# Linear attention before two expert layers: the attention of the last twelve tiles in pairs

## The chip, the cores and the metric

The kernel runs on one core of one Trainium2 chip. The metric is the device time of one execution in microseconds, the median of several runs. One more execution is recorded by the hardware profiler; all rows come from that one.

The engines of a core work side by side, each in its own order, and wait for one another through semaphores: PE (TensorE) multiplies matrices, DVE (VectorE), ACT (ScalarE) and POOL (GpSimd) work element by element, SP (SyncE) issues most DMAs. PEld is the loading of weights into PE's array, which runs beside the products.

## The reference

Three stages, over 4 batches, 8 heads, 768 time steps and head width 48:

```python
# attention, for each batch and head: state is a 48x48 matrix
for t in range(768):
    y[t]  = r[t] @ (state + outer(u * k[t], v[t]))
    state = w[:, None] * state + outer(k[t], v[t])
# x: 3072 rows of 384
h = maximum(maximum(x @ w1, x @ w2), x @ w3);  x = h @ w_out          # width 768
xn = x / rms(x) * rms_g
out = (silu(xn @ w_gate) * (xn @ w_val)) @ w_out2                      # width 1536
```

## The kernel before

**Attention in tiles.** The recurrence is computed in chunks of 128 time steps; a tile `i` is one chunk of one batch, `i = 4*chunk + batch`, 24 tiles in all. For a tile there are, on PE: the scores `pe_a` (L352: eight small products of 48 rows, for four pairs of heads, the two heads of a pair on two halves of the rows, into two PSUM banks), the outputs `pe_y` (L410: products with 32 output columns, four side by side, into one bank) and, but for the last chunk, the state products `pe_st` (L378: 64 output columns, two side by side, one bank). Each product shows as two instructions in the profile. Around them: `prep` scales r and k by the decay (L316, DVE) and forms `ru = r*u*k` (L324 and L325, on DVE for tiles under 8, on POOL later); `prep_b` sums `ru` by head (L332, DVE) and spreads the sums on diagonals (`Dg`, L335, POOL); `mix` copies the masked scores into `Dg` (L359, DVE, two instructions); `fin` takes the outputs out of PSUM (L425 on ACT, L426 on DVE); `mask_kv` takes the state products out (L365, ACT, into the buffer `kv`); POOL decays the state and adds `kv` (L384, L386). From tile 8 on a part of `fin`'s output goes into a buffer `yt` and four DMAs turn it into place (`turn`, L438 and L439).

**Order of the work.** Everything is written out in one order. The first expert layer is cut into `slots` (24 for each chunk `u`; 18 of them are nine products `pl` of 128x512 in one of four PSUM banks `psm`, L99 to L101). Attention is a list of `steps`, three for each tile, which are strewn between the slots: of the stages `u` = 1 to 4 each has 12 steps, and after slot `n` the steps up to number ceil(12 (n+1) / 20) have been issued. After each step one more waiting load is issued. The step `block(i)` holds, in PE's order, scores of tile `i+1`, outputs of tile `i`, states of tile `i`. Other work goes in between: `tick` converts the experts' weights (L137 to L147), `sums_step` forms sums of weights (L168), `later` holds low parts (L498) back by a slot.

**Buffers.** The tags `ru` and `kv` have one buffer each, `yt` one, `Dg` two, `tm` and `raw` (the loaded tile) three. Scores, outputs and state products turn in the four PSUM banks of `psx`. `csb` holds the identity (used once, by the transposes of `tables3`), the mask and two columns. The tag `wf` turns in six buffers of the weight conversion.

After attention the second expert layer runs from products of sums (`px`, `pa`, L1031 and others) to the end.

Of the kernel before, what the change touches and what calls it, by code (L numbers as in the profile page):

```python
# [71 lines left out]
def rwkv_moe_kernel(ctx, tc, rkT, rkv, wd, ub, cst, rg, w1p, wo1p, w2p, out):  # L72
# [154 lines left out]
                    fn(i + off)  # L227


    csb = tp.tile([128, 259], F32, name="csb")  # L230
    ident = csb[:, 0:128]
    cmask = csb[:, 128:256].bitcast(U32)
    m01 = csb[:, 256:257], csb[:, 258:259]
    small = tp.tile([128, 4, NP], F32, name="small")
    wsb, wcl, w128, ok = (small[:, n] for n in range(4))
    usb = tp.tile([128, DM], F32, name="usb")
# [14 lines left out]
    def load_tile(i):  # L251
        if i >= NT:
            return
        a = raws[i % 3][:, :, 0:512].rearrange("p s (q t) -> p s q t", t=128)
        t = tp.tile([128, VO + NP * 144], F32, tag="tm", bufs=3, name=f"tm{i}")
        raw_t[i], tm_t[i] = a, t
        for j in range(2):
            loads.append(lambda j=j: sync.dma_start(a[64 * j:64 * j + 48], rkT[i, 48 * j:48 * j + 48]))
        rk = t[:, 0:2 * KO].rearrange("p (s n) -> p s n", s=2)[:, :, 0:DM]
        loads.append(lambda: sync.dma_start(rk, rkv[i, :, 0:2 * DM].rearrange("p (s n) -> p s n", s=2)))  # L260
        loads.append(lambda: sync.dma_start(t[:, VO:], rkv[i, :, 2 * DM:]))
# [56 lines left out]
    def prep(i):  # L318
        prep_raw(i)
        s = st[i]  # L320
        tm = s["tm"]
        ru = tp.tile([128, DM], F32, tag="ru", name=f"ru{i}")
        eng = dve if i < NRU else pool
        eng.tensor_tensor(out=ru, in0=tm[:, 0:DM], in1=usb, op=ALU.mult)  # L324
        eng.tensor_tensor(out=ru, in0=ru, in1=tm[:, KO:KO + DM], op=ALU.mult)  # L325
        s["ru"] = ru
# [18 lines left out]
    def pe_a(i):  # L345
        s = st[i]
        raw = s["raw"]
        pa = [psx.tile([128, NP, 128], F32, tag="x", name=f"pa{i}_{j}") for j in range(2)]
        for pr in range(NP):
            for j in range(2):  # L350
                sl = slice(64 * j, 64 * j + 48)
                pe.matmul(pa[j][:, pr], raw[sl, 1, pr], raw[sl, 0, pr], start=True, stop=True)  # L352
        s["pa"] = pa

    def mix(i):
        s = st[i]
        dg = s["Dg"].rearrange("p (r j) t -> p r j t", j=2)
        for j in range(2):
            dve.copy_predicated(out=dg[:, :, j], mask=cmask.unsqueeze(1).to_broadcast([128, NP, 128]),  # L359
                                data=s["pa"][j])  # L360
# [3 lines left out]
            sl = slice(48 * j, 48 * j + 48)  # L364
            act.activation(o[:, :, sl], pk, AF.Copy, scale=m01[j])  # L365

    def pe_st(i):
        s = st[i]
        c, b = divmod(i, B)
        if c == NB - 1:  # L370
            return
        tm = s["tm"]
        v3 = tm[:, VO:].rearrange("p (r q e) -> p r q e", q=3, e=D)
        pk = psx.tile([128, NP, D], F32, tag="x", name=f"pkv{i}")
        for pr in range(NP):
            for j in range(2):
                o = KO + 96 * pr + 48 * j
                pe.matmul(pk[64 * j:64 * j + 64, pr], tm[:, o:o + 64], v3[:, pr, 2 * j], start=True, stop=True)  # L378
        if c == 0:
            mask_kv(Tst[b], pk)  # L380
        else:
            kv = tp.tile([128, NP, 96], F32, tag="kv", name=f"kv{i}")
            mask_kv(kv, pk)
            pool.tensor_tensor(out=Tst[b], in0=Tst[b],  # L384
                               in1=w128.unsqueeze(2).to_broadcast([128, NP, 96]), op=ALU.mult)
            pool.tensor_tensor(out=Tst[b], in0=Tst[b], in1=kv, op=ALU.add)  # L386

    def pe_y(i):
        s = st[i]
        c, b = divmod(i, B)  # L390
        tm = s["tm"]
        py = s["py"] = psx.tile([128, 3, 128], F32, tag="x", name=f"py{i}")
        lanes = []
        for n in range(4):
            lane = []
            for k in range(3):
                m = (n + TURN[k] * (i >= TURNED)) % 4
                pr, o = (k, 32 * m) if m < 3 else (3, 32 * k)
                ops = [(tm[:, VO + 144 * pr + 48 * j + o:VO + 144 * pr + 48 * j + o + 32],
                        s["Dg"][:, 2 * pr + j]) for j in range(2) if o != (64, 0)[j]]  # L400
                if c > 0:
                    ops.append((Tst[b][:, pr, o:o + 32], s["raw"][:, 0, pr]))
                for m, (l, r) in enumerate(ops):
                    lane.append((py[32 * n:32 * n + 32, k], l, r, m == 0, m == len(ops) - 1))
            lanes.append(lane)
        for m in range(max(map(len, lanes))):
            for lane in lanes:
                if m < len(lane):
                    o, l, r, start, stop = lane[m]
                    pe.matmul(o, l, r, start=start, stop=stop)  # L410
# [3 lines left out]
    def fin(i):  # L414
        s = st[i]
        u, m = divmod(i, B)
        if m == 0:
            xt[u] = ap_.tile([128, 2, 3, 512], F32R, tag="x", bufs=2, name=f"x{u}")
        xh, xl = xt[u][:, 0], xt[u][:, 1]
        o = 128 * m  # L420
        cs = slice(o, o + 128)
        y = s["py"]

        def split(hi, lo, y):
            act.copy(hi, y)  # L425
            dve.tensor_tensor(out=lo, in0=y, in1=r32(hi), op=ALU.subtract)  # L426

        if i < TURNED:
            split(xh[:, :, cs], xl[:, :, cs], y)
            return  # L430
        t = tp.tile([128, 2, 2, 128], F32R, tag="yt", name=f"yt{i}")
        split(t[:, 0], t[:, 1], y[:, 0::2])
        split(xh[:, 1, cs], xl[:, 1, cs], y[:, 1])

        def turn():
            for n, k in enumerate((0, 2)):
                o = 32 * TURN[k]
                sync.dma_start(r32(xt[u][o:128, :, k, cs]), r32(t[0:128 - o, :, n]))  # L438
                sync.dma_start(r32(xt[u][0:o, :, k, cs]), r32(t[128 - o:128, :, n]))  # L439

        turns.append(turn)
# [1 line left out]
    turns = []  # L443

    def att_steps():
        def block(i):
            if i + 1 < NT:
                pe_a(i + 1)
                mix(i + 1)
            pe_y(i)  # L450
            fin(i)
            pe_st(i)
            load_tile(i + 3)

        def ahead(i):
            while turns:
                turns.pop(0)()
            if i < NT:
                load_next(2)
                prep(i)  # L460

        def ahead_b(i):
            load_next(1)
            prep_b(i)
            prep2(i)

        for i in range(NT):
            yield lambda i=i: block(i)
            yield lambda i=i: ahead(i + 2)
            yield lambda i=i: ahead_b(i + 2) if i + 2 < NT else None  # L470

    hs, sB = {}, {}

# [103 lines left out]
    with tc.manual_schedule():  # L577
# [3 lines left out]
            sync.dma_start(wsb[64 * j:64 * j + 48], wd[48 * j:48 * j + 48])  # L581
        load_tile(0)
        load_next(4)
        sync.dma_start(csb[:, 0:258], cst)
        sync.dma_start(m01[1][16:128], cst[0:112, 257:258])
        sync.dma_start(m01[1][0:16], cst[112:128, 257:258])
        act.dma_start(usb, ub.partition_broadcast(128))
# [725 lines left out]
```

## Time and profile before

| | us |
|---|---|
| median of 3 runs (lowest, highest) | 815.31 (813.35, 815.71) |
| the profiled execution, its own time | 816.15 |
| its span, first to last instruction | 814.4 |
| PE busy in the span | 793.0 |
| DVE busy | 578.6 |
| ACT busy | 427.3 |
| POOL busy | 241.1 |

Busy shares of PE say only that it had work in flight: matmuls overlap, and small ones leave parts of the array and of the time unused while PE counts as busy. A row of the timeline that ends in x16 merges sixteen instructions; the number in brackets is the idle time before it and what ended it.

### The profile page before, as it was taken

The numbers are of one execution on the slowest core, as the hardware profiler recorded it, in microseconds if no ns is written. First come the engines' busy times: TensorE is split into PE (matmuls) and PEld (weight loads), VectorE is DVE, ScalarE is ACT, GpSimd is POOL, SyncE is SP. The second block draws the span as 40 slices with busy tenths as digits, with TensorE's granted clock in tenths as the row PEclk, the third lists the DMA queues.
The fourth block names the chain that finished last, engine by engine and source line by source line (L and its number), as shares of the span: only waits on it lengthen the run. The fifth ranks groups of instructions, "written<-read, shape, count | busy, mean of one in ns | idle before, by whom it ended". The sixth has DMA issues, their size and how long they took to land.

```text
span 814.4 us, 14091 instructions
## 1 busy us (share of the span) xinstructions
PE 793.0 (97%) x5098; PEld 652.2 (80%) x5098; DVE 578.6 (71%) x948; ACT 427.3 (52%) x812; POOL 241.1 (30%) x241
## 2 busy tenths in 40 slices
PE   7799999999999999999999999999999999999996
PEld 6688887888888888888787888788888788888884
DVE  8898979948959748518946679866677884665551
ACT  1998865455453542224576666555444555444431
POOL 2488834544354541013267773000000000000000
PEclk8999999999999999999999999999999999999999
DMA  9996685666475654035279874318454405544211
GB/s 240 272 271 187 222 251 179 187 218 206 136 236 160 211 188 147 20 130 165 87 247 331 282 238 169 118 57 278 139 183 145 130 26 175 157 153 141 73 40 43
DMA packets 83594, 139.28 MB, mean 171 GB/s; under 512 B 10550, under 2 KB 46902, under 8 KB 83516
## 3 DMA queue, kind: packets, MB, share of 16 engines
q1 hardware_dynamic: 80172, 122.37, 48.9%
q0 software_dynamic: 3200, 15.73, 5.1%
q8 instruction: 42, 0.69, 0.4%
q14 instruction: 36, 0.29, 0.1%
q10 hardware_dynamic: 144, 0.20, 0.1%
HBM read 98.65 MB, written 35.41 MB: 165 GB/s over the span
## 4 chain that ended last, share of the span: by engine, by line
PE 84%; DVE 6%; DMA 3%; ACT 3%; issue 2%; SPq 0%; POOL 0%; DVEq 0%; ACTq 0%; POOLq 0%
PE px L99 11%; PE px L100 11%; PE px L101 11%; PE pl L99 8%; PE pl L101 7%; PE pl L100 7%; PE pa L100 5%; PE pa L101 5%; PE pa L99 5%; PE py L410 4%; PE po L100 3%; PE po L99 3%; PE po L101 3%; PE pa L352 2%; DMA raw<-in_rkT 1%
## 5 line engine op out<-in xcount | busy, mean ns | idle before, releaser
L99 PE MATMUL pl<-x,w_a 128*128 128x512 f32 (+1 forms) x342 | 132.0, 386 | 1.4 <-DVE c L495 1.0
L100 PE MATMUL pl<-x,w_a 128*128 128x512 f32 (+1 forms) x342 | 129.6, 379 | 0.7 <-DVE x L426 0.7
L101 PE MATMUL pl<-x,w_a 128*128 128x512 f32 (+1 forms) x342 | 129.6, 379 | 0.5 <-POOL w_a L156 0.5
L99 PEld LDWEIGHTS pl<-x,w_a 128*128 128x128 f32 x342 | 64.3, 188 | 15.0 <-DVE c L495 1.4
L101 PEld LDWEIGHTS pl<-x,w_a 128*128 128x128 f32 x342 | 64.3, 188 | 13.0 <-POOL w_a L156 0.7
L100 PEld LDWEIGHTS pl<-x,w_a 128*128 128x128 f32 x342 | 64.4, 188 | 12.6 <-DVE x L426 1.1
L495 DVE TENSOR_TENSOR c<-pl,c 128x512 f32<-128x512 f32 (+1 forms) x76 | 49.9, 657 | 28.8 <-PE pl L101 26.6
L1031 DVE TENSOR_TENSOR px<-px,sb 128x512 f32<-128x512 f32 x56 | 39.0, 698 | 33.0 <-PE px L101 32.1
L497 ACT CAST h1h<-c 128x512 fp32r<-128x512 f32 (+1 forms) x32 | 19.0, 594 | 82.1 <-DVE c L495 82.0
L147 DVE SCALAR_TENSOR_TENSOR wf<-wf,wraw 128x384 uint32<-128x384 uint32 x60 | 46.3, 775 | 13.1 <-ACT wraw L140 12.6
L335 POOL TENSOR_SCALAR_AFFINE_SELECT Dg<-a 128x1024 f32<-128x1024 f32 x24 | 30.2, 1259 | 80.2 <-DVE a L332 67.2
L1019 ACT COPY sb<-px 128x512 f32<-128x512 f32 x63 | 37.0, 587 | 32.0 <-PE px L101 28.3
L657 POOL TENSOR_TENSOR ws<-wsf,ws 128x384 fp32r<-128x384 f32 x40 | 41.7, 1042 | 40.1 <-ACT ws L656 29.9
L100 PE MATMUL px<-hb,wo 128*128 128x512 f32 x132 | 51.6, 391 | 0.2 <-DVE hb L1017 0.2
L99 PE MATMUL px<-hb,wo 128*128 128x512 f32 x132 | 51.6, 391 | 0.0
L101 PE MATMUL px<-hb,wo 128*128 128x512 f32 x132 | 51.4, 390 | 0.0
L359 DVE COPY_PREDICATED Dg<-csb,pa 128x512 f32<-128x512 uint32 x48 | 32.5, 731 | 20.3 <-PE pa L352 17.1
L410 PE MATMUL py<-Dg,tm 128*32 128x128 f32 x768 | 40.6, 288 | 0.0
L1055 DVE TENSOR_TENSOR hb<-h,hb 128x512 fp32r<-128x512 f32 x36 | 24.9, 691 | 21.8 <-ACT hb L1054 21.6
L139 ACT ACTIVATE wraw<-wraw 128x384 uint16<-128x384 uint32 x60 | 38.9, 648 | 2.0
L140 ACT ACTIVATE wraw<-wf 128x384 f16<-128x384 f32 x60 | 38.7, 645 | 2.0
L137 ACT ACTIVATE wf<-wraw 128x384 f32<-128x384 f32 x60 | 33.5, 558 | 11.2 <-DMA w2o<-wf 10.1
(306 smaller groups left out, 2116.5 us busy)
## 6 DMA issues: line engine op xcount, KB each, us to landing
ws<-w2s SPq DMA_DIRECT2D x80, 384.0 KB, 3.0
w2s<-ws POOLq DMA_DIRECT2D x40, 384.0 KB, 3.5
wraw<-in_w2p SPq DMA_DIRECT2D x36, 384.0 KB, 5.1
raw<-in_rkT SPq DMA_DIRECT2D x48, 192.0 KB, 3.6
tm<-in_rkv SPq DMA_DIRECT2D x24, 384.0 KB, 4.1
wsf<-w2f SPq DMA_DIRECT2D x120, 64.0 KB, 3.2
tm<-in_rkv SPq DMA_DIRECT2D x24, 288.0 KB, 4.4
wraw<-in_w1p SPq DMA_DIRECT2D x18, 384.0 KB, 7.9
```

Source lines behind the costliest of these rows:

```text
L99: pe.matmul(o, lh, rh, start=start, stop=False, **kw)
L100: pe.matmul(o, lh, rl, start=False, stop=False, **kw)
L101: pe.matmul(o, ll, rh, start=False, stop=stop, **kw)
L137: act.activation(w, hi.bitcast(F32), AF.Copy, scale=2.0 ** -112)
L139: act.activation(x[:, :, 0], lo, AF.Copy, scale=2.0 ** -29 * (1 - 2.0 ** -12), bias=-0.4996)
L140: act.activation(x[:, :, 1].bitcast(F16), w, AF.Copy)
L147: dve.scalar_tensor_tensor(out=wu, in0=wu, scalar=3, in1=cbits(n).bitcast(U32), op0=ALU.logical_shift_left, op1=ALU.bitwise_or)
L410: pe.matmul(o, l, r, start=start, stop=stop)
L495: dve.tensor_tensor(out=c1[:, :n], in0=p[:, :n], in1=c1[:, :n], op=ALU.max)
L657: pool.tensor_tensor(out=t[:, :, 1], in0=r, in1=r32(t[:, :, 0]), op=ALU.subtract)
L1019: (act.copy if kind == "e" else dve.tensor_copy)(get(ks[1]), get(ks[0]))
L1031: dve.tensor_tensor(out=o, in0=a, in1=b, op=op)
```

## The change

From tile 12 on, attention is issued in pairs of tiles. `block` is gone; `scores` issues the score products of all its tiles and then their mixes, `outputs` the output products of all its tiles, their `fin`, their state products and then the state updates. Tiles 1 to 11 keep their order, written as `scores(i + 1), outputs(i)`; the scores of tiles 12 and 13 come with the step `ahead_b(13)`. After that six steps serve two tiles: `outputs` of the pair, `ahead` and `ahead_b` for each tile of the next pair, `scores` of the next pair. The state products of a pair share one PSUM bank. `yt` gets two buffers. `ru` and `kv` share one buffer, the tag `rk`. The identity moves into a buffer of the tag `wf` and has a DMA of its own.

```diff
@@ -227,10 +227,10 @@
                     fn(i + off)
 
 
-    csb = tp.tile([128, 259], F32, name="csb")
-    ident = csb[:, 0:128]
-    cmask = csb[:, 128:256].bitcast(U32)
-    m01 = csb[:, 256:257], csb[:, 258:259]
+    csb = tp.tile([128, 131], F32, name="csb")
+    ident = cp.tile([128, 128], F32, tag="wf", bufs=6, name="ident")
+    cmask = csb[:, 0:128].bitcast(U32)
+    m01 = csb[:, 128:129], csb[:, 130:131]
     small = tp.tile([128, 4, NP], F32, name="small")
     wsb, wcl, w128, ok = (small[:, n] for n in range(4))
     usb = tp.tile([128, DM], F32, name="usb")
@@ -319,7 +319,7 @@
         prep_raw(i)
         s = st[i]
         tm = s["tm"]
-        ru = tp.tile([128, DM], F32, tag="ru", name=f"ru{i}")
+        ru = tp.tile([128, DM], F32, tag="rk", name=f"ru{i}")
         eng = dve if i < NRU else pool
         eng.tensor_tensor(out=ru, in0=tm[:, 0:DM], in1=usb, op=ALU.mult)
         eng.tensor_tensor(out=ru, in0=ru, in1=tm[:, KO:KO + DM], op=ALU.mult)
@@ -364,22 +364,30 @@
             sl = slice(48 * j, 48 * j + 48)
             act.activation(o[:, :, sl], pk, AF.Copy, scale=m01[j])
 
-    def pe_st(i):
+    def pe_st(i, pk=None):
         s = st[i]
         c, b = divmod(i, B)
         if c == NB - 1:
             return
         tm = s["tm"]
         v3 = tm[:, VO:].rearrange("p (r q e) -> p r q e", q=3, e=D)
-        pk = psx.tile([128, NP, D], F32, tag="x", name=f"pkv{i}")
+        if pk is None:
+            pk = psx.tile([128, NP, D], F32, tag="x", name=f"pkv{i}")
         for pr in range(NP):
             for j in range(2):
                 o = KO + 96 * pr + 48 * j
                 pe.matmul(pk[64 * j:64 * j + 64, pr], tm[:, o:o + 64], v3[:, pr, 2 * j], start=True, stop=True)
+        s["pk"] = pk
+
+    def state(i):
+        c, b = divmod(i, B)
+        if c == NB - 1:
+            return
+        pk = st[i]["pk"]
         if c == 0:
             mask_kv(Tst[b], pk)
         else:
-            kv = tp.tile([128, NP, 96], F32, tag="kv", name=f"kv{i}")
+            kv = tp.tile([128, NP, 96], F32, tag="rk", name=f"kv{i}")
             mask_kv(kv, pk)
             pool.tensor_tensor(out=Tst[b], in0=Tst[b],
                                in1=w128.unsqueeze(2).to_broadcast([128, NP, 96]), op=ALU.mult)
@@ -428,7 +436,7 @@
         if i < TURNED:
             split(xh[:, :, cs], xl[:, :, cs], y)
             return
-        t = tp.tile([128, 2, 2, 128], F32R, tag="yt", name=f"yt{i}")
+        t = tp.tile([128, 2, 2, 128], F32R, tag="yt", bufs=2, name=f"yt{i}")
         split(t[:, 0], t[:, 1], y[:, 0::2])
         split(xh[:, 1, cs], xl[:, 1, cs], y[:, 1])
 
@@ -443,14 +451,25 @@
     turns = []
 
     def att_steps():
-        def block(i):
-            if i + 1 < NT:
-                pe_a(i + 1)
-                mix(i + 1)
-            pe_y(i)
-            fin(i)
-            pe_st(i)
-            load_tile(i + 3)
+        def scores(*tiles):
+            for i in tiles:
+                pe_a(i)
+            for i in tiles:
+                mix(i)
+
+        def outputs(*tiles):
+            for i in tiles:
+                pe_y(i)
+            for i in tiles:
+                fin(i)
+            pk = None
+            if len(tiles) > 1 and tiles[0] // B < NB - 1:
+                pk = psx.tile([128, 2, NP, D], F32, tag="x", name=f"pkv{tiles[0]}")
+            for n, i in enumerate(tiles):
+                pe_st(i, pk if pk is None else pk[:, n])
+            for i in tiles:
+                state(i)
+                load_tile(i + 3)
 
         def ahead(i):
             while turns:
@@ -460,14 +479,24 @@
                 prep(i)
 
         def ahead_b(i):
-            load_next(1)
-            prep_b(i)
-            prep2(i)
-
-        for i in range(NT):
-            yield lambda i=i: block(i)
+            if i < NT:
+                load_next(1)
+                prep_b(i)
+                prep2(i)
+
+        for i in range(11):
+            yield lambda i=i: (scores(i + 1), outputs(i))
             yield lambda i=i: ahead(i + 2)
-            yield lambda i=i: ahead_b(i + 2) if i + 2 < NT else None
+            yield lambda i=i: ahead_b(i + 2)
+        yield lambda: outputs(11)
+        yield lambda: ahead(13)
+        yield lambda: (ahead_b(13), scores(12, 13))
+        for i in range(12, NT, 2):
+            yield lambda i=i: (outputs(i, i + 1), load_next(2))
+            for j in (i + 2, i + 3):
+                yield lambda j=j: ahead(j)
+                yield lambda j=j: ahead_b(j)
+            yield lambda i=i: scores(i + 2, i + 3) if i + 2 < NT else None
 
     hs, sB = {}, {}
 
@@ -581,7 +610,8 @@
             sync.dma_start(wsb[64 * j:64 * j + 48], wd[48 * j:48 * j + 48])
         load_tile(0)
         load_next(4)
-        sync.dma_start(csb[:, 0:258], cst)
+        sync.dma_start(ident, cst[:, 0:128])
+        sync.dma_start(csb[:, 0:130], cst[:, 128:258])
         sync.dma_start(m01[1][16:128], cst[0:112, 257:258])
         sync.dma_start(m01[1][0:16], cst[112:128, 257:258])
         act.dma_start(usb, ub.partition_broadcast(128))
```

## Rows read from the trace of the kernel before

**Rows 1.** Profile page, part 1: span and busy time of the engines.

```profile
span 814.4 us, 14091 instructions
...
PE 793.0 (97%) x5098; PEld 652.2 (80%) x5098; DVE 578.6 (71%) x948; ACT 427.3 (52%) x812; POOL 241.1 (30%) x241
```

**Rows 2.** Waits of PE, 56 us to the end: total us, times, longest.

```profile
PE pl L99 <- DVE c L495: 1.0, 1, 1.0
```

**Rows 3.** Windows view: us; PE, PEld, DVE, ACT, POOL busy; clock; DMA share; GB/s.

```profile
173.10:237.10 64.00, 64.00 (x571) 52.49 (x570) 51.46 (x100) 29.84 (x61) 28.96 (x26) 1.00 0.62 187
```

**Rows 4.** Timeline of the weight loads around block 13: start, us, line, count.

```profile
186.14 0.19 PEld L100 LDWEIGHTS pl<-x,w_a 128*128 128x128 f32 x1
186.37 0.19 PEld L101 LDWEIGHTS pl<-x,w_a 128*128 128x128 f32 x1
186.91 0.97 PEld L352 LDWEIGHTS pa<-raw 48*128 48x128 f32 x16 [0.35 <-issue]
188.00 0.25 PEld L410 LDWEIGHTS py<-Dg,tm 128*32 128x32 f32 x9
...
189.23 0.24 PEld L410 LDWEIGHTS py<-raw,T 128*32 128x32 f32 x8
189.66 0.55 PEld L378 LDWEIGHTS pkv<-tm 128*64 128x64 f32 x16 [0.20 <-issue]
190.27 0.19 PEld L568 LDWEIGHTS ss<-srh,ones 128*128 128x128 f32 x1
190.37 0.19 PEld L569 LDWEIGHTS ss<-srl,ones 128*128 128x128 f32 x1
```

**Rows 5.** Timeline of the weight loads around block 23.

```profile
340.39 0.19 PEld L101 LDWEIGHTS pl<-x,w_a 128*128 128x128 f32 x1
340.93 0.25 PEld L410 LDWEIGHTS py<-Dg,tm 128*32 128x32 f32 x9 [0.35 <-issue]
...
342.15 0.24 PEld L410 LDWEIGHTS py<-raw,T 128*32 128x32 f32 x8
342.59 0.19 PEld L99 LDWEIGHTS pl<-x,w_a 128*128 128x128 f32 x1 [0.20 <-issue]
```

**Rows 6.** Lines L410 and L378, 170 to 345 us: waits of PE's sequencer.

```profile
L410 PEldq EVENT_SEMAPHORE  x11: 51/51/51, 173.1 to 336.8; - x11
...
L378 PEldq EVENT_SEMAPHORE  x8: 51/51/51, 175.1 to 281.0; - x8
```

**Rows 7.** Timelines of PE and DVE around block 15: products y15, mix 16.

```profile
216.05 0.42 PE L410 MATMUL py<-Dg,tm 128*32 128x128 f32 x7
...
219.92 1.34 DVE L359 COPY_PREDICATED Dg<-csb,pa 128x512 f32<-128x512 uint32 x2
```

**Rows 8.** Timelines of POOL and DVE around 70 us: state sum, ru product.

```profile
70.01 1.89 POOL L386 TENSOR_TENSOR T<-T,kv 128x384 f32<-128x384 f32 x1
...
70.94 1.38 DVE L324 TENSOR_TENSOR ru<-tm,usb 128x384 f32<-128x384 f32 x1
```

**Rows 9.** Chain of waits at its start: start, us, engine, tile.

```profile
9.48 0.48 DVE ru L324
...
14.01 1.11 DVE raw L316
```

**Rows 10.** Timeline of SyncE's DMA queue: constants, then loads and turns after block 12.

```profile
4.58 0.43 SPq L584 DMA_DIRECT2D csb<-in_cst  x1
...
6.07 1.21 SPq L258 DMA_DIRECT2D raw<-in_rkT  x2
...
177.69 0.63 SPq L438 DMA_DIRECT2D x<-yt  x1
...
181.65 0.47 SPq L261 DMA_DIRECT2D tm<-in_rkv  x1
```

**Rows 11.** Profile page, part 6: DMA issues, KB each, us to landing.

```profile
tm<-in_rkv SPq DMA_DIRECT2D x24, 288.0 KB, 4.4
```

**Rows 12.** Waits of all engines, 170 to 345 us: total, times, longest.

```profile
ACT x L425 <- DVE yt L426: 11.2, 12, 3.1
```

## The prediction

> **What bounds the kernel now.** I read the busy times first: PE is in flight 793.0 of 814.4 us and no other engine comes near [rows 1]. Busy says little for PE, so the waits come next: from 56 us to the end PE's longest wait is 1.0 us, for a DVE maximum that frees a bank [rows 2]. In the stage of tiles 12 to 15 PE never idles, its clock is full (1.00), and DVE with 51.46 of 64.00 us has room in the mean [rows 3]. So only what shortens PE's own stream can shorten the time, and what the change adds elsewhere costs nothing until PE waits.
>
> PE's stream is read from the weight loads, since a load shows when PE could take up the next product. Large products follow each other every 0.23 us (186.14, 186.37). The next load was due at 186.60 and came at 186.91: entering small products costs 0.31. The eight score pairs have their loads 0.11 apart ((0.97 - 0.19) / 7), so the outputs were due at 187.80 and came at 188.00: 0.20. The last two rows of four outputs, 0.11 apart, begin at 189.23, so the states were due at 189.45 and came at 189.66: 0.21. The states' pitch is 0.06 ((0.55 - 0.13) / 7, with 0.13 for the last load as in the row above it), so the large products were due at 190.13 and came at 190.27: 0.14. Of the entry, 0.13 is won back there, as the first two loads stand 0.10 apart instead of 0.23 [rows 4]. Block 23, which has outputs alone, shows the two other passages: entry at 340.93 for 340.62, 0.31, and from outputs back to large products 342.59 for 342.37, 0.22 [rows 5]. Every change of kind thus has a gap of 0.14 to 0.31 us, while within one kind there is none.
>
> **The change part by part.** *Pairs.* It removes no product; it removes passages. From block 11 on, before: 12 passages from scores to outputs (12 x 0.20 = 2.40), 9 from outputs to states (1.89), 4 from outputs to large products (0.88), 9 from states to large products (1.26): 6.43 us. Entries are 13 (12 with scores, block 23 without). After: entries are 13 again (outputs of tile 11, six scores, six outputs), so they cancel. The others: 5 from outputs to states (1.05), 5 from states to large products (0.70), 2 from outputs to large products (0.44), and 6 from scores to large products, which no row shows. Its bounds are 0.14 and 0.31, the smallest and the largest gap seen; I take 0.20, the gap that follows scores now. That makes 1.20, and 3.39 together. The gain is 6.43 - 3.39 = 3.0 us, from 2.4 to 3.4 by the unknown passage.
>
> Are the gaps a property of the passage, or are they waits for semaphores? PE's sequencer shows its waits as instructions of 0.051 us. At the outputs the last of them is at 336.8 us, yet block 23 at 340.93 has the full gap; at the states there is one for each of 8 tiles [rows 6], a quarter of the 0.21. So the rows speak for the passage. Second tiles of a pair keep their waits: six scores, six outputs, four states, 16 x 0.051 = 0.8 us if none is hidden. I take nothing, since the sequencer runs ahead of the array, and keep 0.8 as a bound.
>
> The Trainium skill, TensorEngine Tiling (Array Packing), section Key Properties, has a rule for it: changing the tiling mode drains TensorE, changing only the tile does not. By it the passages go from 47 to 31 and the joined tiles cost nothing; if the gaps were waits that each tile keeps, nothing would be gained.
>
> *Mixes.* The scores of a pair now run after slot 8 or 18, the outputs after slot 10 or the next stage's slot 0. The close case is 8 to 10, three times (tiles 14, 18, 22). From the end of the first tile's scores PE has the second scores (0.89), the passage (0.20), 18 large products (4.1), less 0.13, and an entry (0.31): 5.4 us until it needs the first mix, which takes 1.34. DVE may begin it 4.0 us late. The largest lag among the mixes of tiles 13 to 23 is that of tile 16, 219.92 - 216.05 = 3.9 us [rows 7]. The second mix has 1.34 more to do, but is needed 1.5 later (14 rows of 0.11). So no wait, with 0.1 us to spare in the worst lag seen. Nothing is taken; behind a late mix DVE holds its maxima, and PE's banks with them.
>
> *One buffer for ru and kv.* New waits. First, for tiles 6 and 7, DVE's `ru` waits for POOL's state sum. For tile 7 the sum ends at 70.01 + 1.89 = 71.90, and `ru` began at 70.94: up to 1.0 us later [rows 8]. But it took 1.38 while POOL ran, and 0.48 where POOL was silent [rows 9]: 71.90 + 0.48 = 72.38 against 72.32. I take 0.1 for the two, with 0 and 2.0 as bounds. Behind it queue DVE's maxima, for which PE waits later [rows 2]. Second, in a pair ACT's `mask_kv` of the second tile waits for POOL's sum of the first, up to 1.9 us by the same row [rows 8]. Behind it stand ACT's copies from `psm`; ACT has already sat 3.1 us between its two parts of `fin` [rows 12] with no wait of PE. Priced at nothing; with only one free bank it would cost its 1.9 us four times. Third, the first tile's `mask_kv` waits for the second's states in the shared bank, 0.5 us, under the same cover.
>
> *Loads.* SyncE issues after a pair's outputs three loads of the next but one tile ahead of eight turns. A turn takes 0.63 to issue, a load 0.47 to 0.61, and a load lands 4.4 after it [rows 10, 11]: 1.7 + 4.4 = 6.1 us. The scaling of that tile comes five slots of nine products later, at 10.3. The second `yt` buffer hides no wait of these rows and costs nothing. If a load came late, DVE would stand before its maxima.
>
> *Identity.* One more DMA at the start, 0.43 us of SyncE's queue, in front of tile 1's loads. Those were issued by 7.28; with 0.43 and 4.4 they land by 12.1, and DVE takes them at 14.01 [rows 9, 10, 11]. Nothing. The buffer is free for the conversion that gets it long after the transposes.
>
> **The sum.** 3.0 - 0.1 = 2.9 us, so the span goes from 814.4 to 811.5, the profiled execution's own time from 816.15 to 813.2, and the median, which lies 0.8 under that execution, from 815.3 to 812.4. What a measurement of this kernel can tell is about 0.3%, 2.4 us, so a gain counts below 812.9.
>
> **Rivals.** *A part given back.* The second tiles' semaphores show (0.8), the unknown passage is 0.31 (0.6 less), DVE's wait for POOL costs 1.0: a gain of 0.5 to 2.4, some 814.0. For it: that stretch of DVE ends in the one wait of PE [rows 2]. Against it: it needs two of the three.
>
> *Pairing does not shorten PE's stream.* If each tile, not each passage, carries the gap, the time stays at 815.3. For it: the profile calls these gaps issue and names no releaser [rows 4]. Against it: the gap without a semaphore, and that none is seen between products of one kind.
>
> *The mix comes late.* At slot 10 PE stands at `pe_y` of tiles 14, 18 and 22. It decides from a lag of 4.0 us; to be slower by 2.4 beyond the lost 2.9 it must take 1.8 us in each of three places, a lag of 5.8; 818 us. For it: the worst lag is 3.9, sums of weights and the mixes of two tiles now stand together on DVE, and there are half as many stretches of small products in which DVE catches up. Against it: DVE has a fifth of the stage free [rows 3].
>
> The Trainium skill speaks for this rival: TensorEngine Tiling (Array Packing), Gotcha 1: PSUM Pressure, has row tiles write to different banks. So the scores of a pair fill all four banks of `psx`, and the outputs get theirs only from the mixes. No run here shows yet what that costs.
>
> **How the numbers follow.** The forecast, gain 2.4 to 3.5, 812.4: 0.54. A part given back, 814.0: 0.26. No shorter stream, 815.3: 0.12. Late mixes, 818: 0.08. Alone the forecast has 811.8 to 812.9. The range to 815.4 takes in the second case and half of the third; below, 811.4 allows the larger gain and the measurement's spread. Faster by over 0.3%: nearly all of the forecast, 0.52; slower: the last, 0.08; within: 0.40.
>
> **What would show it.** Right: stretches of scores alone and of outputs of two tiles; no gap between tiles of a pair; 31 passages; no wait of PE at L410; 343 us (the end of attention on PE) about 3 us earlier. Wrong: a wait of PE at L410 for DVE's mix after slot 10, a larger wait at L99 for DVE near 128 us, or gaps between the tiles of a pair as large as between kinds.

## The result and the profile after

The changed kernel takes 823.62 us (median of 6 runs, 823.03 to 825.62) where the kernel before takes 815.47 (6 runs, 813.35 to 816.24): ratio 1.0101, with an interval of 1.0090 to 1.0112. It is 1% slower. Forecast were 812.4 us, in a range from 811.4 to 815.4. The profiled execution took 823.63 us, 7.5 more than that of before, and its span is 7.5 longer too.

The page of the changed kernel, part 1, answers to [rows 1]:

```profile
span 821.9 us, 14102 instructions
...
PE 796.1 (97%) x5098; PEld 655.7 (80%) x5098; DVE 580.4 (71%) x948; ACT 429.0 (52%) x812; POOL 240.0 (29%) x241
```

PE has 3.1 us more in flight and 4.4 us more without work. Its waits from 56 us to the end, in the same view as [rows 2] (total us, times, longest), say for what:

```profile
PE pl L99 <- DVE c L524: 7.1, 5, 2.4
PE pl L99 <- ACT c L521: 0.7, 1, 0.7
```

In before there was one such wait of 1.0 us. Now there are six, 7.8 us in all, and none at `pe_y`, the place that the prediction had watched. Two come early (0.73 at 120.2 us, 1.11 at 129.7) and four in the stages of the pairs, 6.0 us in all, the longest of 2.44 and 2.42.

**What the pairs gained.** The timeline of the weight loads around the outputs of tiles 12 and 13 and the scores of 14 and 15 answers to [rows 4]:

```profile
175.44 0.25 PEld L418 LDWEIGHTS py<-Dg,tm 128*32 128x32 f32 x9 [0.35 <-issue]
...
176.66 0.24 PEld L418 LDWEIGHTS py<-raw,T 128*32 128x32 f32 x8
176.88 0.33 PEld L418 LDWEIGHTS py<-Dg,tm 128*32 128x32 f32 x9
...
178.63 1.01 PEld L379 LDWEIGHTS pkv<-tm 128*64 128x64 f32 x32 [0.20 <-issue]
179.70 0.19 PEld L99 LDWEIGHTS pl<-x,w_a 128*128 128x128 f32 x1
...
201.33 1.86 PEld L352 LDWEIGHTS pa<-raw 48*128 48x128 f32 x32 [0.36 <-issue]
203.31 0.19 PEld L99 LDWEIGHTS pl<-x,w_a 128*128 128x128 f32 x1
```

The outputs of two tiles run in one stretch: the last rows of the first tile begin at 176.66 and the second tile 0.22 later, which is their own length, so there is no gap. The outputs take 3.19 us together, the states 1.07, and the scores 1.98 where two tiles took 2 x 1.09. The passage that no row had shown, from scores to large products, costs 0.20, as taken: sixteen pairs of 0.111 us ((1.86 - 0.19) / 15) make 1.78 of the 1.98. Added over all stretches of small products from block 11 on, PE spends 40.17 us in before and 37.65 after: a gain of 2.5 us.

**What took it back.** The timeline of PE around the first long wait, then the windows of the same stretch and of the stage of [rows 3] (columns as there):

```profile
192.68 0.39 PE L101 MATMUL pl<-x,w_a 128*128 128x512 f32 x1
195.50 0.80 PE L99 MATMUL pl<-x,w_a 128*128 128x512 f32 x1 [2.44 <-DVE c L524]
196.10 0.63 PE L100 MATMUL pl<-x,w_a 128*128 128x512 f32 x1
```

```profile
193.10:195.60 2.50, 0.10 (x1) 0.10 (x1) 2.36 (x4) 0.00 (x0) 1.52 (x2) 0.94 0.93 352
195.60:198.00 2.40, 2.40 (x6) 1.92 (x7) 2.40 (x4) 1.72 (x4) 0.00 (x0) 0.50 0.89 334
198.00:201.00 3.00, 3.00 (x13) 2.38 (x12) 1.60 (x3) 1.60 (x3) 2.17 (x2) 0.88 0.39 41
...
173.10:237.10 64.00, 61.49 (x556) 50.47 (x555) 52.66 (x100) 29.59 (x59) 27.92 (x26) 0.97 0.60 182
```

PE stands for 2.44 us for the DVE copy `c` (L524, it takes the maximum) that frees a bank. After it the granted clock is 0.50, the lower of its two levels (1.2 GHz). The products come 0.43 us apart instead of 0.23: from 195.50 the next seven take until 198.66, 3.16 us instead of 1.59, so 1.6 us more are lost. The wait of 2.42 at 263.62 goes the same way. In the windows view of before the stage had PE busy all the time at clock 1.00 [rows 3].

The balance: 6.8 us more of these waits, 3.2 for the two stretches at half clock, 2.5 less for passages, and a wait of 0.55 us at 436.6 (for ACT's `sb`) that is absent, together 6.9. The waits view counts from the end of the work in flight. By the starts of the products a wait delays PE 0.15 more (195.50 comes for 192.91, 2.59 late, where 2.44 are counted); there are four more waits than in before, so that is another 0.6. So 7.5 are found for 7.5.

**Why DVE is late for PE now.** A bank of `psm` is wanted again four groups of products later. Take that of slot 4 in the stage that starts at 173 us: behind it come slot 5, the two products `ss`, slot 6, and slot 7, which takes the bank of slot 4. In before, PE's timeline around block 13:

```profile
184.55 0.39 PE L101 MATMUL pl<-x,w_a 128*128 128x512 f32 x1
...
186.91 1.16 PE L352 MATMUL pa<-raw 48*128 48x128 f32 x16
...
190.27 0.50 PE L568 MATMUL ss<-srh,ones 128*128 128x512 f32 x1
...
192.90 0.39 PE L99 MATMUL pl<-x,w_a 128*128 128x512 f32 x1
```

and DVE's:

```profile
188.78 0.29 DVE L168 TENSOR_TENSOR wf<-wf,wf 128x128 f32<-128x128 f32 x1
189.11 0.29 DVE L186 SCALAR_TENSOR_TENSOR wf<-wx,wf 128x128 f32<-128x128 f32 x1
189.32 1.48 DVE L495 TENSOR_TENSOR c<-pl,c 128x512 f32<-128x512 f32 x2
```

Slot 4's last product starts at 184.55. Its maximum comes only at 189.32, because six weight sums, a low part, a reduction and a conversion stand in front of it; the bank is free at 190.00. But block 13's small products, 186.91 to 190.27, write into `psx`, not `psm`. PE is busy with them while DVE catches up, and it wants slot 4's bank again only at 192.90, 2.90 us after it is free. In the changed kernel nothing of the kind stands between slot 0 (small products of two tiles, to 179.70) and slot 8 (scores from 201.33). DVE's timeline there, and POOL's:

```profile
184.82 1.10 DVE L168 TENSOR_TENSOR wx<-wf,wf 128x128 f32<-128x128 f32 x1
185.96 0.91 DVE L168 TENSOR_TENSOR wf<-wf,wf 128x128 f32<-128x128 f32 x1
...
192.94 0.97 DVE L168 TENSOR_TENSOR wf<-wf,wf 128x128 f32<-128x128 f32 x1
193.94 0.91 DVE L186 SCALAR_TENSOR_TENSOR wf<-wx,wf 128x128 f32<-128x128 f32 x1
194.77 1.48 DVE L524 TENSOR_TENSOR c<-pl,c 128x512 f32<-128x512 f32 x2
```

```profile
183.90 1.88 POOL L324 TENSOR_TENSOR ru<-tm,usb 128x384 f32<-128x384 f32 x1
185.85 0.86 POOL L325 TENSOR_TENSOR ru<-ru,tm 128x384 f32<-128x384 f32 x1
...
192.71 1.04 POOL L324 TENSOR_TENSOR ru<-tm,usb 128x384 f32<-128x384 f32 x1
193.84 0.86 POOL L325 TENSOR_TENSOR ru<-ru,tm 128x384 f32<-128x384 f32 x1
```

The bank comes free at 195.46 (194.77 + 0.69), and PE wanted it at 192.91. Counted from the first large product behind slot 0 (176.46 before, 179.70 after), PE comes 3.23 us earlier (13.21 instead of 16.44) and DVE frees the bank 2.22 later (15.76 instead of 13.54): 2.90 - 3.23 - 2.22 = -2.55, and PE starts 2.59 late. The sum also says that the two parts need each other: by it PE's earlier coming alone would have made a short wait (0.3 us), and DVE's delay alone none.

DVE's delay has rows too. The four sums shown took 0.28 or 0.29 each in before (two of them in the rows above) and take 1.10, 0.91, 0.97 and 0.91 now, and each ends 0.14 to 0.16 us after the POOL instruction beside it (183.90 + 1.88 = 185.78, the sum at 185.92). POOL forms `ru` there; in the first case it has the state updates of two tiles in front of it. The Trainium skill, SBUF — State Buffer, section SBUF: two separate sides, says that GpSimd and a VectorE instruction with two inputs in SBUF share a pair of ports that one of them holds for a whole instruction while the other is blocked. The rows agree: the sums end as if they had stood until POOL's instruction was over.

### The profile page after: what moved, and what is told of

Read it like the earlier page. It is cut to its first block, busy times and chain, and to the rows that moved or that the text cites. A ratio compares the mean times of both kernels' runs of the same rounds, so it can differ in the third digit from the quotient of the medians.

```text
span 821.9 us, 14102 instructions
## 1 busy us (share of the span) xinstructions
PE 796.1 (97%) x5098; PEld 655.7 (80%) x5098; DVE 580.4 (71%) x948; ACT 429.0 (52%) x812; POOL 240.0 (29%) x241
## 4 chain that ended last, share of the span: by engine, by line
PE 78%; DVE 10%; ACT 5%; issue 3%; DMA 2%; POOL 1%; SPq 1%; DVEq 0%; ACTq 0%; POOLq 0%
PE px L99 11%; PE px L100 11%; PE px L101 11%; PE pl L99 6%; PE pl L100 6%; PE pl L101 6%; PE pa L100 5%; PE pa L101 5%; PE pa L99 5%; PE py L418 3%; PE po L99 3%; PE po L100 3%; PE po L101 3%; DVE wf L168 2%; PE pa L352 2%
## 5 line engine op out<-in xcount | busy, mean ns | idle before, releaser
L99 PE MATMUL pl<-x,w_a 128*128 128x512 f32 (+1 forms) x342 | 134.3, 393 | 10.2 <-DVE c L524 7.1
L100 PE MATMUL pl<-x,w_a 128*128 128x512 f32 (+1 forms) x342 | 131.3, 384 | 0.6 <-DVE x L434 0.6
L101 PE MATMUL pl<-x,w_a 128*128 128x512 f32 (+1 forms) x342 | 130.8, 382 | 0.0
L99 PEld LDWEIGHTS pl<-x,w_a 128*128 128x128 f32 x342 | 65.3, 191 | 26.4 <-DVE c L524 9.2
L100 PEld LDWEIGHTS pl<-x,w_a 128*128 128x128 f32 x342 | 65.6, 192 | 12.5 <-DVE x L434 1.0
L101 PEld LDWEIGHTS pl<-x,w_a 128*128 128x128 f32 x342 | 65.5, 191 | 12.6
L524 DVE TENSOR_TENSOR c<-pl,c 128x512 f32<-128x512 f32 (+1 forms) x76 | 49.9, 657 | 33.9 <-PE pl L101 33.1
L418 PE MATMUL py<-Dg,tm 128*32 128x128 f32 x768 | 40.4, 287 | 0.0
L137 ACT ACTIVATE wf<-wraw 128x384 f32<-128x384 f32 x60 | 33.4, 557 | 10.0 <-DMA wraw<-in_w2p 5.0
L418 PEld LDWEIGHTS py<-Dg,tm 128*32 128x32 f32 x768 | 33.7, 114 | 4.5 <-issue 2.7
```

The source lines that it names most:

```text
L99: pe.matmul(o, lh, rh, start=start, stop=False, **kw)
L100: pe.matmul(o, lh, rl, start=False, stop=False, **kw)
L101: pe.matmul(o, ll, rh, start=False, stop=stop, **kw)
L137: act.activation(w, hi.bitcast(F32), AF.Copy, scale=2.0 ** -112)
L524: dve.tensor_tensor(out=c1[:, :n], in0=p[:, :n], in1=c1[:, :n], op=ALU.max)
```

## The experiments

Two theories. *Place*: the time is lost because the small products moved from between the slots to slot 0 and slot 8, so that PE returns to a `psm` bank before DVE has emptied it. *Crowding*: it is lost because POOL's work for two tiles stands together and slows DVE. A third question is apart from both: what the buffer edits cost by themselves. The expectations call these theories A, B and C. The first two do not exclude each other, and by the sum above both are at work. All ratios are against the kernel before, run on the same chip.

**1. Outputs and scores of the pairs three steps later** (changed kernel; outputs after slots 5 and 15, scores after 3 and 13).

```diff
+        for _ in range(3):
+            yield lambda: None
         for i in range(12, NT, 2):
```

> Three empty steps stand before the first pair, so that the outputs of a pair come after slots 5 and 15 of a stage instead of 0 and 10, and the scores after slots 3 and 13. Theory A (place): in the changed kernel PE waits at L99 for DVE's maxima at slot 7 (2.44 us at 195.50, 2.42 at 263.62), because the small products that stood after slot 5 in the kernel before (3.4 us, at 186.91) gave DVE the time to free the banks and now stand after slot 0. Then the waits of PE at L99 between 170 and 350 us fall from 6.0 us to under 1, the clock stays at 1.00, and the time is 812 to 814. Theory B (crowding): the waits come because POOL's state sums of two tiles and the ru products stand in one row and slow DVE's sums of weights (0.28 us each alone, 0.8 to 1.1 beside POOL). They stay in one row, so 3 us or more of waits stay, 818 or more. Theory C (the shared and moved buffers): no change, 823.6.

818.42 us, ratio 1.0032 (1.0022 to 1.0042): 5 us of the 8 come back, and the 812 to 814 of theory A are missed. Its waits of PE:

```profile
PE pl L99 <- DVE c L526: 2.6, 1, 2.6
PE pa L352 <- DVE raw L316: 0.7, 1, 0.7
PE py L418 <- DVE Dg L359: 0.7, 3, 0.3
PE py L418 <- issue: 0.7, 2, 0.5
```

The wait of 2.6 is at 121 us, in the stage ahead of the pairs, and the clock is 0.50 behind it, from 122 to 124 us; this run doesn't explain the size of the wait. After 170 us no wait for a maximum is left, as *place* expects. In its stead stand the waits of the prediction's late mix: in this order the outputs follow the scores so closely that PE stands at L418 for `Dg`, and at L352 for scaled rows. Three of the six joined outputs took 3.7 to 3.8 us instead of 3.2.

**2. The buffer edits alone** (kernel before, tiles one by one).

```diff
...
-        ru = tp.tile([128, DM], F32, tag="ru", name=f"ru{i}")
+        ru = tp.tile([128, DM], F32, tag="rk", name=f"ru{i}")
...
-            kv = tp.tile([128, NP, 96], F32, tag="kv", name=f"kv{i}")
+            kv = tp.tile([128, NP, 96], F32, tag="rk", name=f"kv{i}")
...
-        t = tp.tile([128, 2, 2, 128], F32R, tag="yt", name=f"yt{i}")
+        t = tp.tile([128, 2, 2, 128], F32R, tag="yt", bufs=2, name=f"yt{i}")
...
-        sync.dma_start(csb[:, 0:258], cst)
+        sync.dma_start(ident, cst[:, 0:128])
+        sync.dma_start(csb[:, 0:130], cst[:, 128:258])
```

> The kernel before with the edits of buffers alone: identity in a conversion buffer with its own DMA, one buffer for ru, k and state sums, two buffers yt; attention tile by tile as before. Theories A and B: at most the wait of PE near 128 us grows (in the changed kernel 0.73 + 1.11 us before 150 us, where the kernel before has 0.98), 815.3 to 816.5. Theory C: most of the 8 us shows here, 820 or more.

817.30 us, ratio 1.0019 (1.0009 to 1.0029): 0.7 to 2.4 us slower. PE has two early waits, 0.93 at 120.9 and 1.09 at 130.5, as in the changed kernel.

**3. The pairs' places, but outputs, states and updates tile by tile.**

```diff
             for i in tiles:
                 pe_y(i)
+                fin(i)
+                pe_st(i)
+                state(i)
             for i in tiles:
-                fin(i)
...
-            for n, i in enumerate(tiles):
-                pe_st(i, pk if pk is None else pk[:, n])
-            for i in tiles:
-                state(i)
                 load_tile(i + 3)
```

> The changed kernel, but in the outputs of a pair each tile has its outputs, its fin, its states and its state update before the next tile begins, with a bank each for the states; the place of everything stays. Theory of the passages: two passages come back in each of four pairs (states to outputs and outputs to states, some 0.2 us each) and the gap between two tiles' outputs in the two last pairs: 1.5 to 2 us more on PE, which may be hidden where PE waits for DVE anyway, 823.6 to 825.5. If the gaps belonged to the tiles, no change of PE's small products: 823.6 with equal stretches (4.27 us for the outputs and states of a pair). Theory B, in the order of POOL: the first tile's state sum comes 1 us earlier, waits change by under 1 us.

823.76 us, ratio 1.0089 (1.0069 to 1.0109), which can't be told from the changed kernel. The long waits are there again (1.94 and 2.40), with clock 0.50 behind each. Passages given back are hidden behind them, so this run tells nothing of their price; run 12 does.

**4. POOL's decay and sum of the states left out from tile 12 on.**

```diff
+            if i >= 12:
+                return
             pool.tensor_tensor(out=Tst[b], in0=Tst[b],
```

> The changed kernel without POOL's decay of the state and without its state sum (L392, L394) for tiles from 12 on, so the outputs of later chunks lack these tiles; some 4 us of POOL less after each pair. Theory B: DVE's maxima after a pair come 2 us or more earlier, the waits of PE at L99 from 170 us on fall from 6.0 us to under 2, and the clock stays at 1.00: 814 to 816. Theory A alone: DVE's lag falls by under 1 us, the waits stay above 4 us, 820 to 823.

819.07 us, ratio 1.0039 (1.0028 to 1.0051). The waits after 170 us are 0.91, 1.92 and 0.42 us, 3.2 instead of 6.0, and the clock stays at 1.00. That is between the two theories (under 2 and above 4 were expected). The rows of its first long wait, from the timelines of DVE and PE, part the two:

```profile
192.39 1.47 DVE L526 TENSOR_TENSOR c<-pl,c 128x512 f32<-128x512 f32 x2
```

```profile
193.12 0.50 PE L99 MATMUL pl<-x,w_a 128*128 128x512 f32 x1 [0.91 <-DVE c L526]
```

The first large product behind slot 0 starts at 179.19 here. The bank of slot 4 is free at 193.07, 13.88 us later, which is only 0.34 more than in before (13.54); but PE wants it at 192.06, after 12.87 us instead of 16.44. So *place*, with hardly any delay of DVE, leaves a wait of 1 us here, and POOL's state updates were most of DVE's 2.22. *Crowding* is a part, and not the whole: without it the small products are still missing between the slots.

**5. Two steps later** (outputs after slots 3 and 13, scores after 11 and 1).

```diff
+        for _ in range(2):
+            yield lambda: None
```

> Two empty steps before the first pair: outputs after slots 3 and 13, scores after slots 11 and 1, so the mixes go to DVE before most of the weight sums of a stage and the outputs give DVE 4.6 us before the banks of slots 4 and 5 are wanted. If the place of the small products decides, the waits at L99 after 170 us stay under 1 us, as with three steps, and the waits for mixes (L418, 1.4 us with three steps) shrink under 0.5: 814.5 to 816.5, where 814.6 is the time before, less 2.5 of passages, with 1.8 for the edits of the buffers. If the mixes or the loads come late wherever the pair stands, 818 or more, with waits at L418 or L352.

821.41 us, ratio 1.0053 (1.0029 to 1.0077). No wait for a maximum after 170 us, as in run 1, but a long new one (and two of 0.4 and 0.5 us for low parts, L529). Its timelines of DVE and PE, and the window behind the wait:

```profile
206.99 0.17 DVE L571 TENSOR_SCALAR n<-n 128x8 f32<-128x8 f32 x1 [5.98 <-DMA n<-msd]
...
209.38 0.54 DVE L332 TENSOR_REDUCE a<-ru 128x8 f32<-128x384 f32 x1
...
213.07 2.56 DVE L359 COPY_PREDICATED Dg<-csb,pa 128x512 f32<-128x512 uint32 x4
```

```profile
213.88 1.22 PE L418 MATMUL py<-Dg,tm 128*32 128x128 f32 x10 [4.00 <-issue]
```

```profile
213.80:217.00 3.20, 3.12 (x50) 2.55 (x54) 3.20 (x6) 2.21 (x4) 0.00 (x0) 0.50 0.42 128
```

DVE stood 5.98 us for a DMA of the norm (`n`), issued at 202.79. That one waited 1.9 us for another (`msd`), which SyncE issued only at 199.38, behind the eight turns and three loads, though ACT had its row done at 193.2. The sum by head (L332), POOL's spread and the mixes came late behind it; PE stood 4.00 us at L418, then ran the outputs at clock 0.50. This is the rival of the late mix, with a DMA as its cause, and the time expected if the place decides (814.5 to 816.5) is missed by it.

**6. Two weight sums at a time instead of four, everywhere** (changed kernel).

```diff
-                sums_step(4)
+                sums_step(2)
```

> The changed kernel with two instead of four weight sums let through after each slot. A maximum then stands behind half as many sums on DVE. If PE waits because DVE's maxima of slots 4 and 5 stand behind the sums, the waits at L99 after 170 us fall from 6.0 us to under 2, the clock stays at 1.00 (no idle time over 1 us), and the time is 815 to 818. If POOL's crowding alone slows DVE, whatever it does, 3 us or more of the waits stay, 819 or more.

815.77 us, ratio 0.9998 (0.9987 to 1.0009). No product is moved; only what stands ahead of a maximum on DVE becomes shorter. No wait of PE is left after 170 us. A wait of 1.5 us at 146.7 is new: the sums end later, the DMAs that store them come later too, and ACT stands 4.7 us for one (before L137), with its copy out of a bank behind it.

**7. The shared buffer of `ru` and `kv` alone** (kernel before; the first two edits of run 2).

> The kernel before with one buffer for ru and kv and nothing else. With all edits of buffers together 1.8 us were lost; there DVE's ru of tile 7 begins right when POOL's state sum ends (73.51), 2 us later on its way than in the kernel before. If that wait carries the loss, 816.5 to 817.5, with a second wait of PE at L99 near 121 us; if the moved identity, its DMA or the second yt buffer carries it, 815.3 and one wait near 128 us.

816.91 us, ratio 1.0011 (1.0001 to 1.0022). DVE's timeline shows the waits of tiles 6 and 7, and PE's waits what they do:

```profile
59.91 1.08 DVE L324 TENSOR_TENSOR ru<-tm,usb 128x384 f32<-128x384 f32 x1 [0.91 <-POOL T L386]
...
73.36 1.34 DVE L324 TENSOR_TENSOR ru<-tm,usb 128x384 f32<-128x384 f32 x1 [0.91 <-POOL T L386]
```

```profile
PE pl L99 <- DVE c L495: 2.0, 2, 1.1
```

So this edit carries the second early wait of PE. What the identity's DMA and the second `yt` buffer add in run 2 is within the intervals, and stays open.

**8. Ten of the sixteen sums of each set of weights left out from stage 2 on** (changed kernel).

```diff
...
+            if stage[0] < 2 or any(out is x for x in (E1, E2, E3, E4, E5, E6)):
...
```

> The changed kernel with ten of the sixteen sums of each set of weights left out from stage 2 on (the weights of the second layer are then not the right ones); POOL and the place of everything are kept. If PE waits for a DVE that is behind with its sums, the waits at L99 after 170 us go to under 0.5 us and the clock stays at 1.00: 814 to 816, that is the 814.6 of the time before less the passages plus the edits of the buffers. If something else holds the banks (ACT's copies, the wait of the second mask_kv for POOL), the waits stay.

815.52 us, ratio 0.9988 (0.9975 to 1.0001). No wait for a maximum after 170 us. With run 6: it is DVE's work ahead of the maximum that counts. The two runs' times can't be told apart; both have waits of their own elsewhere (2.5 us in two early ones here).

**9. The pairs mended** (changed kernel; `kv` of tiles 4 to 7 takes a buffer of `yt`, which is free then, and the sums come by two from stage 2 on).

```diff
-            kv = tp.tile([128, NP, 96], F32, tag="rk", name=f"kv{i}")
+            kv = (tp.tile([128, NP, 96], F32, tag="yt", bufs=2, name=f"kv{i}") if i < TURNED
+                  else tp.tile([128, NP, 96], F32, tag="rk", name=f"kv{i}"))
...
-                sums_step(4)
+                sums_step(4 if u < 2 else 2)
```

> The changed kernel with two edits: the kv of tiles 4 to 7 lie in the yt buffers (free until tile 8), so DVE's ru of tiles 6 and 7 no longer waits for POOL's state sum; and from stage 2 on two weight sums instead of four follow each slot. If the time before lost only to these two waits, PE waits at L99 near 128 us as before (1.0 us, and no longer near 121), nowhere between 170 and 350 us, and the shorter stretches of small products remain: 2.5 us, so 812.5 to 813.5 beside 815.5 to 816 of the kernel before (ratio 0.997). If the edits of the buffers lose elsewhere, or the loss of the changed kernel only moves, ratio 1.000 or more.

812.82 us (12 runs), ratio 0.9969 (0.9956 to 0.9982): faster than both. The early waits are 1.5 us, with one of 0.37 left near 119 us where none was expected. Its waits of PE, and the window of the stages with pairs (columns as in [rows 3]):

```profile
PE pl L99 <- DVE c L525: 1.5, 2, 1.1
```

```profile
170.00:345.00 175.00, 175.00 (x1575) 145.55 (x1574) 129.47 (x252) 79.55 (x158) 66.27 (x58) 1.00 0.55 165
```

**10. The same rule for the sums, kernel before.**

```diff
-                sums_step(4)
+                sums_step(4 if u < 2 else 2)
```

> The kernel before with two instead of four weight sums after each slot from stage 2 on, nothing else. From stage 2 on PE does not wait for DVE in the kernel before, so every theory has it unchanged: ratio 0.999 to 1.001. If it becomes faster, the gain of the mended pairs is not that of the pairs.

815.44 us, ratio 1.0000 (0.9989 to 1.0011). So run 9's gain is that of the pairs, not of the rule. Nor is it that of the other buffer for `kv`, which only undoes a wait: the early waits of run 9 (1.5 us) are no less than the 1.0 of before.

**11. Useless work where the small products stood** (changed kernel; fifteen products of 128x512, 3.4 us, after slot 5 of stages 2 and 3, into a bank of `psx`).

```diff
+                if u in (2, 3) and n == 5:
+                    idle = psx.tile([128, 512], F32, tag="x", name=f"idle{u}")
+                    for _ in range(15):
+                        pe.matmul(idle, ones, xt[u][:, 0, 0], start=True, stop=True)
```

> The changed kernel with fifteen useless products of 128x512 (3.4 us of PE, into a bank of psx that nobody reads) after slot 5 of stages 2 and 3, where the small products of an odd block stood before. Theory of the place: PE has 6.8 us more to do, yet the time does not grow: the two long waits (2.44 and 2.42 us, 0.73 before the second) and the stretches of half clock behind them (1.6 us each) go, 8.8 us in all, 820.5 to 823.6. If PE's waits do not hang on what PE does after slot 5, the time grows by about 6.8: 829 to 831.

824.34 us (4 runs), ratio 1.0108 (1.0089 to 1.0126). PE's waits from 170 to 345 us, and the window of the stage:

```profile
PE pl L99 <- DVE c L524: 0.4, 1, 0.4
```

```profile
173.10:237.10 64.00, 64.00 (x576) 53.23 (x575) 52.19 (x99) 30.97 (x61) 28.45 (x26) 1.00 0.60 182
```

PE does 6.8 us more, and the time rises by 0.7 over the changed kernel's (from ratio 1.0101 to 1.0108). The waits of that stretch are 0.4 us instead of 6.0, and the clock stays at 1.00. By waits and clock 821.6 was due (823.6 + 6.8 - 5.6 - 3.2); the early waits are 0.7 longer in this execution, and there is one of 1.2 for `sb` late in the run, which leaves about 1 us open. What matters: work of no use, put at that place, is nearly free. So *place* is shown as a cause that the waits can't do without. That it is the only one is not shown: POOL's work stands together here as before, and run 4 shows what that adds.

**12. Run 9, tile by tile** (its two edits and that of run 3).

> The mended pairs, but with outputs, states and state update of each tile of a pair in turn, as in the earlier run tile by tile, where PE's waits may have hidden the difference. No waits are left here, so the passages show: in each of four pairs two more (0.2 us each) and in the two last pairs a second row of outputs that begins alone; 1.5 to 2 us over the mended pairs, 814 to 815.5. If the gaps belonged to the tiles, the same time as the mended pairs.

814.20 us (12 runs), ratio 0.9984 (0.9974 to 0.9994). With nothing to hide behind, the passages show. Its weight loads around tiles 12 and 13:

```profile
174.34 0.25 PEld L419 LDWEIGHTS py<-Dg,tm 128*32 128x32 f32 x9 [0.35 <-issue]
...
176.00 0.55 PEld L379 LDWEIGHTS pkv<-tm 128*64 128x64 f32 x16 [0.20 <-issue]
176.61 0.25 PEld L419 LDWEIGHTS py<-Dg,tm 128*32 128x32 f32 x9
...
178.27 0.55 PEld L379 LDWEIGHTS pkv<-tm 128*64 128x64 f32 x16 [0.20 <-issue]
178.88 0.19 PEld L99 LDWEIGHTS pl<-x,w_a 128*128 128x128 f32 x1
```

Outputs, states, outputs, states take 174.34 to 178.88, 4.54 us, where the joined ones of the changed kernel take 175.44 to 179.70, 4.26. The difference, 0.28, occurs four times: 1.1 us of PE (in the two last pairs, which have no states, nothing changes, 3.19); the medians are 1.4 apart (their intervals overlap, so the rows carry this and the medians only agree). Here the rule that the prediction quoted, TensorEngine Tiling (Array Packing), section Key Properties, in the Trainium skill (a change of the mode drains TensorE, a change of the tile does not) agrees with the trace: the same products cost 0.28 more with two more changes of kind.

## Why the prediction was wrong

*Pairs.* Right in kind and nearly in size: 31 passages, no gap between tiles of a pair, the unknown passage 0.20 as taken, 2.5 us for 3.0 (bounds 2.4 and 3.4). The shortfall is for the most part in the joined outputs, which take 0.08 more than the working made of them (3.19 for twice 1.45 and 0.21), six times. The second tiles' semaphores, one of the three parts of the rival of a part given back, don't show: there is no gap at 176.88. The rival that pairing does not shorten PE's stream falls with run 12.

*"What the change adds elsewhere costs nothing until PE waits."* The step that failed stands behind this sentence. PE's next wait was looked for in one place, `pe_y` after slot 10 (the part on mixes), and for the rest the mean of a stage was taken as proof of room: DVE with 51.46 of 64.00 us [rows 3]. The banks of `psm` were not worked out, though the one wait of before was of that kind [rows 2] and the small products that gave DVE its time could be seen in [rows 4]. The move of small products was priced at nothing. It was worth 3.23 us at a place with 2.90 us to spare, and 2.22 us of DVE's delay came on top; the next stage repeats it. The rival of the late mix even names that "there are half as many stretches of small products in which DVE catches up", but prices it only in mixes. The working that was missing takes rows of before alone: when DVE frees the bank (190.00), when PE wants it (192.90), and how much of what lies between is moved (186.91 to 190.27). It would have shown a wait of some 0.5 us (3.36 moved, 2.90 to spare); for the rest of it, POOL's order would have had to be worked out too.

*A wait's price.* The rivals counted a wait by its length. The two long ones cost 1.6 us more each, for the products behind them at half clock.

*One buffer for `ru` and `kv`.* Mis-sized. Each `ru` waited 0.91 us, within the "up to 1.0" of the text; but 0.1 was taken for both, on the argument that `ru` is quick once POOL is silent. POOL went on with other work, and `ru` took 1.08 and 1.34 in run 7, the next instruction 1.25 and 0.56. Counted from the scaling in front (L316), DVE was done with the two 0.95 us later than in before for tile 6 and 0.25 later for tile 7, 1.2 for the 0.1. The edit cost 0.1 to 1.8 us (run 7), within the bounds 0 to 2.0. The wait of ACT's `mask_kv` for POOL (1.24 us in the second tile) was taken without a wait of PE, rightly: the one wait of PE for ACT, 0.73 at 258.9, is for a copy that itself stood 1.6 us for DVE's low part `h1l` (L527).

*Mixes.* No wait at L418 in the changed kernel, as forecast, but not for the reason given. The largest lag in before is not the 3.9 of tile 16: the mix of tile 18 begins at 256.48 for scores that ended at 252.02, 4.5 us late, and by the working's own limit of 4.0 PE would have stood. In the changed kernel DVE was idle, waiting for the scores, ahead of each of the three close mixes (0.39 us at 202.53, 270.70 and 333.25), so the lags of before did not carry over. How little room there is shows in runs 1 and 5, where the outputs follow the scores in another place and PE waits at L418.

*Loads and identity* made no row of their own.

With the two failed terms mended, the sum comes out: run 9 gains 2.5 us by its ratio (1.5 to 3.6) where 2.9 were forecast. That agrees with the working of the rest. How the mended gain divides between the two edits of run 9 stays open: run 6 has the sums alone, but in the stage before the pairs too, where it made a wait of its own. A run that takes away half clock and leaves the waits was not made.

## What to carry to other kernels

Before small work is moved on the engine that bounds a kernel, list for each bank behind the old place when it is freed and when it is wanted again: work that fills no such bank is the time in which the next engine catches up, and joining it takes that time away. A mean busy share says nothing of that. Where the order is to change all the same, shorten what stands ahead of the instruction that frees the bank; spreading the weight sums from stage 2 on cost nothing by itself (run 10) and, with the other buffer for `kv`, let the pairs gain what they had in them (run 9).

## What the runs showed of the hardware

Half clock followed the idle stretches of 2.44 and 2.42 us of PE and lasted about 3 us. It followed those of 1.94 and 2.40 in run 3 as well, but only 0.8 to 1.0 us after PE had gone on (products about 0.4 us apart from 197.18 and from 265.44), that of 2.60 in run 1, and that of 4.00 in run 5. In run 4 PE idled 1.92 us, in a stretch that is otherwise alike, and the clock stayed up, as timeline and window show:

```profile
258.22 0.50 PE L99 MATMUL pl<-x,w_a 128*128 128x512 f32 x1 [1.92 <-DVE c L526]
```

```profile
258.20:261.00 2.80, 2.78 (x12) 2.33 (x13) 2.73 (x4) 2.01 (x4) 0.00 (x0) 1.00 0.97 368
```

These runs don't show what decides it. I had also not expected that a 128x128 sum on DVE takes over three times as long beside POOL (0.28 alone, 0.91 to 1.10 us in the rows above), where a product of three times the size took 0.48 alone [rows 9]: here what ran beside a sum weighed more than its size.
